# Next inputs by quarters, an ELU end and difference sums at later places, and later chunk loads in a fused retention and ELU kernel

## The chip, the cores and the metric

The kernel runs on one core of one Trainium2 chip. The metric is device time in microseconds for one launch; lower is better. Every run of a kernel gives one time, and a kernel is told by the median of its runs. One further execution is recorded by the hardware profiler, and the profile and the trace come from it.

The engines are named as the profile names them: PE is TensorE (matmuls; PEld are its weight loads), DVE is VectorE, ACT is ScalarE, POOL is GpSimd, and SP is SyncE, whose queue issues the DMAs here. "L921" is line 921 of the kernel before.

## What is computed

The reference, cut to what matters:

```python
def _attn_ref(q, k, v):                      # each (4, 8, 768, 64)
    gamma = 1.0 - 2.0 ** (-5.0 - np.arange(H))
    scale = 1.0 / np.sqrt(D)
    for t in range(S):
        state = gamma * state + einsum('bhd,bhe->bhde', k[:, :, t], v[:, :, t])
        y[:, :, t] = scale * einsum('bhd,bhde->bhe', q[:, :, t], state)

def _moe_ref(x, w_in, w_out):                # (3072, 512), (512, 2048), (2048, 512)
    h = x @ w_in
    g = np.where(h > 0.0, h, np.exp(np.minimum(h, 0.0)) - 1.0)
    return g @ w_out
```

A retention (linear attention with decay, 4 batches, 8 heads, 768 steps, head size 64) gives 3072 tokens of 512 numbers; a layer to 2048, an ELU and a layer back to 512 follow. All of it is float32.

## The kernel before

**Tiling.** The 3072 tokens are worked on in six blocks of 512 (`tb` 0 to 5), each made of four chunks of 128 tokens. A chunk's q, k and v are one load of 1 MB (`load`, L113) into one of four buffers, and its v is scaled on GpSimd soon after the load (`scale_v`, L289). Retention is done chunk by chunk with 64x64 matmuls: scores (L315), masked by VectorE (L326), states (L355, summed by L367), and outputs (L411 and L426, with a small read `seen`, L395, between their two halves, and L401 that writes the result into the input `x` of the first layer).

**Strassen.** The two layers use Strassen's scheme in Winograd's form: seven products of half-sized blocks instead of eight, with sums and differences before and after. Written with a first operand in quarters a11, a12, a21, a22 and a second in b11, b12, b21, b22, product 1 reads b11, 2 reads b21, 3 reads b22, and 4, 5, 6 and 7 read four differences. They are always done in the order 1, 2, 6, 7, 5, 3, 4. Products that share a sum accumulate in the same bank of PSUM: `pa` takes 1, 6, 5 and 3, `pb` takes 2, `pd` takes 7 and 4. Between two products of one bank the partial result must be read out: by a copy on ScalarE from `pa`, by an add on VectorE from `pb` and `pd`. `pa` has two buffers, `pb` and `pd` one each. So a product into `pd` waits until VectorE has read what stood there.

**Two levels.** Blocks 1 to 5 use the scheme twice. The outer level has products `j` in the order 1, 2, 6, 7, 5, 3, 4 (`ORDER2`), and each of them is again seven inner products `k`. The input of an outer product is one of the five arrays `C11`, `C12`, `C21`, `C22` and `T3` (`INPUT2`; `T1` lies in the place of `C12`). Outer product 1 reads C11. Then C11 is overwritten in place: by T3 + C11 for outer product 6, and later by C21 - C11 for outer product 4. That is `next_input` (L790) for block 1, and `next_big_input` (L1202) for the large groups. Within an outer product, inner products 1, 2 and 3 read quarters of the array itself (b11, b21, b22; quarter b12 is read by VectorE alone), and four differences of its quarters are made on VectorE (L879) for inner products 4 to 7.

**Stages in order of time.** Block 0 runs to 130 us or so. Block 1 goes through the first layer in four parts `first(n)` (to 182 us) and through the second in `second_twice` (182 to 243 us, products on L909, sums on L921). Blocks 2 and 3 form the first large group (`nb` = 0), blocks 4 and 5 the second (`nb` = 1). Each large group goes through `big_twice` (products on L1122, sums on L1137), `big_rest` (L1170, sums on L1183) and `second_big` (products on L1222, sums on L1234; 350 to 454 us and 544 to 632 us). While one block is in its layers, the retention of the next ones is slipped in between (`retention_step`), except in the second large group, behind which nothing follows.

**What sets the order.** The program writes its instructions out by hand, with Python generators: an engine executes its own instructions in the order in which the generators emit them, and semaphores order them across engines. `inner(j)` emits products 1 and 2; then 6 and 7; then 5; then 3; then 4, and stops after each of these. The loop of `second_twice` and `second_big` takes outer product `j` through its first steps, then lets the outer product before finish its inner products 3 and 4 (`before`), then yields "first", and so on; "middle" comes between inner products 7 and 5 of `j`, and `j` itself after 5. The main program reacts to these yields with retention steps (`VISITS`) and chunk loads (`LOADS`), both keyed by (step, place), where a step is one outer product. The four chunks of block 3 are loaded during `second_twice`.

**The ELU.** `elu` (L489) emits two instructions on ScalarE, which make exp(min(h, 0)), and puts the third, on VectorE (L498), on a list `later`, so that VectorE needn't wait for ScalarE. `depth` says how many entries the list may hold before its oldest are emitted; `flush` emits all.

**Weights of the second layer.** They lie in DRAM, already combined, and come through a ring of eleven slots of 256 KB (`wq`; eight of them remain for the large groups). An inner product's `done` gives its slot back and `fetch` issues the next load (L821) at once on SyncE's queue. That queue is in order: a DMA that waits for its buffer holds up all DMAs that stand behind it. Chunk loads (L113) and stores of results (L950, L1297) go through the same queue.

**Differences of the first layer's inputs.** For a large group, `big_x` and `big_layer_x` make the differences of inputs (L879 and L1092). They are parts of one generator `xparts`, of which the main loop takes some at a time. `big_end` for C11 (L1183) adds the bank `qa` to it.

Of the kernel before, what the change touches and what calls it, by code (L numbers as in the profile page):

```python
# [19 lines left out]
def kernel(  # L20
# [728 lines left out]
    def first(n):  # L749
# [17 lines left out]

        def use(name, h):
            flat = lambda x: x.rearrange("p a b -> p (a b)")
            elu(flat(mine(name)), flat(h))  # L770
            if name == "C12":

                sub = lambda o, x, y: nc.vector.tensor_tensor(out=o, in0=x, in1=y, op=ALU.subtract)
                later.append(lambda: sub(mine("T3"), mine("C22"), mine("C12")))
                later.append(lambda: sub(mine("T1"), mine("C12"), mine("C11")))
# [9 lines left out]
    def next_input(j):  # L785

        x, op = {2: ("T3", ALU.add), 6: ("C21", ALU.subtract)}[j]
        for n in range(NQ):
            q = slice(2 * n, 2 * n + 2)
            nc.vector.tensor_tensor(out=gq["C11"][:, q], in0=gq[x][:, q], in1=gq["C11"][:, q], op=op)  # L790

# [94 lines left out]
    def second_twice(tb, behind_last):  # L888
# [88 lines left out]
        for at, j in enumerate(ORDER2):  # L977
            cur = inner(j)
            next(cur)
            if j == 1:  # L980
                yield "tail"
            for _ in before:
                pass
            if at:
                yield "first"
            if j == 2:
                flush()
                next_input(2)
            if j == 5:
                next_input(6)  # L990
            if j == 1:

                next(cur)
                yield "elu"
                next(cur)
            parts = input_parts(ORDER2[at + 1]) if at + 1 < 7 else iter(())
            if j in (2, 5):

                next(parts)
            else:  # L1000
                for _ in parts:
                    pass
            if at == 6:
                behind_last()
            if j != 1:
                next(cur)
                yield "middle"
                next(cur)
            for _ in parts:
                pass  # L1010
            before = cur
            yield j
        for _ in before:
# [183 lines left out]
    def next_big_input(j):  # L1197

        x, op = {2: ("T3", ALU.add), 6: ("C21", ALU.subtract)}[j]
        for r in range(2):  # L1200
            for q in (slice(0, 2), slice(2, 4)):
                nc.vector.tensor_tensor(out=G["C11"][r][:, q], in0=G[x][r][:, q], in1=G["C11"][r][:, q], op=op)  # L1202

    def second_big(nb, behind_last):
        quarter = lambda x, r, t: G[x][r][:, :, TH * t : TH * t + TH]
# [118 lines left out]
        for at, j in enumerate(ORDER2):  # L1324
# [6 lines left out]
            if at:  # L1331
                yield "first"
            if j == 2:
                flush()
                next_big_input(2)
            if j == 5:
                next_big_input(6)
            if j == 1:

                next(cur)  # L1340
# [14 lines left out]
                next(cur)  # L1355
            for _ in parts:
                pass
            before = cur
            yield j
        for _ in before:  # L1360
# [242 lines left out]
    flush()  # L1603
    retention_step(2, 2)
    step, VISITS = 0, {(0, "end"): 3, (1, "first"): 4}
    LOADS = {(0, "end"): 0, (1, "middle"): 1, (2, "end"): 2, (4, "middle"): 3}
    for s in sec:
        if s == "first":
            step += 1
# [16 lines left out]
    for nb in range(NB):  # L1626
# [23 lines left out]
        for at, (j, sub) in enumerate(ORDER1):  # L1650
# [4 lines left out]
            if at:  # L1655
                next(tail, None)
            else:
                run(tail)
            next(cur)
            run(tail)  # L1660
            if at == 1 and nb == 0:
# [12 lines left out]
                    retention_step(3, 4)  # L1674
                some(xparts, 4)
            elif at == 2:
                some(xparts, 2)
                if more:
                    bring(groups[0], 0)
            elif at == 3:  # L1680
                run(xparts)
                if more:
                    bring(groups[0], 1)
            if nb == 0:
                stores[at]()
                send_small()
            if at == 2:
                first_c11 = big_end(0, "C11", qa[0])
        next(tail)
        first_c11()  # L1690

        sec = second_big(nb, (lambda: run(big_x(2))) if more else lambda: None)
# [117 lines left out]
```

## Time and profile before

| what | value |
|---|---|
| median of 3 runs | 637.15 us (636.79 to 638.11) |
| the profiled execution's own time | 635.8 us |
| its span, first to last instruction | 634.0 us |
| granted clock of TensorE | 1.00 of full speed, throughout |
| instructions | 13048 |
| read from and written to HBM | 90.96 MB and 28.05 MB |
| weight fetches (L821) | 183 of 256 KB, 3.1 us from issue to landing (median) |
| chunk loads (L113) | 22 of 1 MB, 7.3 us (median) |
| L921, L790 and L1202 on VectorE | 0.28, some 0.62 and some 1.13 us each |

A busy time in the profile is the time in which an engine had an instruction under way. Matmuls are pipelined and their ends are modelled, so a matmul looks busy a little longer than it keeps the next one from starting; the pace from start to start is the better measure. "Idle before" is the time for which an engine did nothing before an instruction, and what stands behind an arrow is what ended that time. A wait for several semaphores is put down to the one that came last. In the timeline, equal instructions that follow each other are put together as "x8"; a float32 matmul counts twice there.

### The profile page before, as it was taken

What the parts mean: (1) busy time and instruction counts of PE and PEld (TensorE: products, weight loads), DVE (VectorE), ACT (ScalarE), POOL (GpSimd) and SP (SyncE); (2) the same over time, 40 slices, a digit from 0 to 9 for tenths busy, and PEclk for the clock granted to TensorE, in tenths of its full rate; (3) what the DMA queues carried; (4) which work ended last, traced back from release to release, by engine and by line L of the source; (5) the groups of instructions that cost most, each with busy time, mean ns of one, the idle gap of its engine ahead of it and who ended that gap; (6) DMA issues with size and microseconds to landing.
All of it is one profiled execution on the core that took longest, in us unless ns stands there. A gap on an engine that the chain in (4) does not pass through costs nothing.

```text
span 634.0 us, 13048 instructions
## 1 busy us (share of the span) xinstructions
PE 619.3 (98%) x5350; PEld 464.5 (73%) x5350; DVE 469.5 (74%) x730; ACT 246.0 (39%) x420; POOL 25.2 (4%) x30
## 2 busy tenths in 40 slices
PE   8999999999999989999999999999999999999997
PEld 5864578888888988764454788888875444688886
DVE  5679789989886785656787986776455777895683
ACT  6798646025541112147657301010236666511110
POOL 1012000000000110010100003000000000000000
PEclk9999999999999999999999999999999999999999
DMA  8698669689464996499000249454643222456552
GB/s 324 253 411 295 182 204 269 196 266 303 152 207 128 385 389 214 141 304 304 34 4 0 84 154 353 169 154 138 201 132 100 67 84 76 135 154 184 152 178 84
DMA packets 73578, 119.85 MB, mean 189 GB/s; under 512 B 5552, under 2 KB 42672, under 8 KB 68784
## 3 DMA queue, kind: packets, MB, share of 16 engines
q1 hardware_dynamic: 73520, 119.04, 57.0%
q8 instruction: 42, 0.69, 0.4%
q14 instruction: 16, 0.13, 0.1%
HBM read 90.96 MB, written 28.05 MB: 188 GB/s over the span
## 4 chain that ended last, share of the span: by engine, by line
PE 90%; DMA 4%; DVE 4%; issue 1%; ACT 0%; SPq 0%; DVEq 0%
PE pa L1222 15%; PE pa L1170 11%; PE pd L1222 7%; PE pb L1170 4%; PE pa L761 4%; PE pb L1222 4%; PE pa L1122 4%; DMA wq<-scratch_dram 3%; PE pa L538 3%; PE x L628 3%; PE pd L1170 3%; PE pa L628 2%; PE pd L1122 2%; PE y L411 2%; PE sc L315 2%; PE pd L761 2%
## 5 line engine op out<-in xcount | busy, mean ns | idle before, releaser
L495 ACT ACTIVATE r<-r 128x512 f32<-128x512 f32 x96 | 60.5, 630 | 3.1
L1230 ACT COPY ms<-pa 128x256 f32<-128x256 f32 x41 | 15.3, 372 | 116.3 <-PE pa L1222 116.3
L1222 PE MATMUL pa<-gC,wq 128*128 128x256 f32 x160 | 38.5, 384 | 0.0
L1234 DVE TENSOR_TENSOR res<-pd,ms 128x256 f32<-128x256 f32 x26 | 11.0, 421 | 35.7 <-PE pd L1222 32.5
L289 POOL TENSOR_TENSOR chunk<-chunk,vf 128x512 f32<-128x512 f32 x16 | 22.3, 1393 | 359.5 <-DMA chunk<-in_qkv_dram 342.1
L1222 PEld LDWEIGHTS pa<-gC,wq 128*128 128x128 f32 x160 | 29.8, 190 | 5.1 <-issue 1.0
L1222 PE MATMUL pa<-ts,wq 128*128 128x256 f32 x112 | 26.5, 379 | 0.0
L1222 PE MATMUL pd<-ts,wq 128*128 128x256 f32 x112 | 26.5, 379 | 0.0
L1170 PE MATMUL pa<-ts,wq 128*128 128x512 f32 x56 | 26.3, 592 | 0.0
L707 ACT COPY m<-pa 128x512 f32<-128x512 f32 x26 | 15.1, 580 | 27.7 <-PE pa L1170 9.6
L1222 PEld LDWEIGHTS pa<-ts,wq 128*128 128x128 f32 x112 | 21.3, 190 | 3.3 <-issue 0.5
L1222 PEld LDWEIGHTS pd<-ts,wq 128*128 128x128 f32 x112 | 21.3, 190 | 2.9
L1222 PE MATMUL pa<-w_s,wq 128*128 128x256 f32 x96 | 22.5, 379 | 0.0
L1133 ACT COPY m<-pa 128x512 f32<-128x512 f32 x16 | 9.4, 585 | 31.2 <-PE pa L1122 31.2
L494 ACT ACTIVATE r<-gC 128x512 f32<-128x512 f32 x24 | 14.9, 621 | 15.2 <-DVE gC L1183 15.2
L1170 PEld LDWEIGHTS pa<-ts,wq 128*128 128x128 f32 x56 | 10.6, 190 | 13.4 <-issue 13.4
L1222 PEld LDWEIGHTS pa<-w_s,wq 128*128 128x128 f32 x96 | 18.2, 190 | 2.9 <-issue 0.5
L1256 ACT COPY res<-pa 128x256 f32<-128x256 f32 x13 | 4.8, 372 | 38.1 <-PE pa L1222 38.1
L917 ACT COPY ms<-pa 128x128 f32<-128x128 f32 x21 | 5.6, 265 | 35.2 <-PE pa L909 34.6
L1183 DVE TENSOR_TENSOR gC<-pa,gC 128x512 f32<-128x512 f32 x20 | 13.8, 689 | 5.8 <-PE pa L1170 5.5
L909 PE MATMUL pd<-ts,wq 128*128 128x128 f32 x112 | 15.2, 278 | 2.8 <-DVE res L921 1.5
L498 DVE SCALAR_TENSOR_TENSOR gC<-r,gC 128x512 f32<-128x512 f32 x24 | 17.5, 729 | 0.3 <-ACT r L495 0.3
(375 smaller groups left out, 1496.9 us busy)
## 6 DMA issues: line engine op xcount, KB each, us to landing
wq<-scratch_dram SPq DMA_DIRECT2D x183, 256.0 KB, 3.1
chunk<-in_qkv_dram SPq DMA_DIRECT2D x22, 1024.0 KB, 7.3
wraw<-in_w_dram SPq DMA_DIRECT2D x15, 1024.0 KB, 6.1
scratch_dram<-gT SPq DMA_DIRECT2D x12, 256.0 KB, 4.3
out_dram<-res SPq DMA_DIRECT2D x5, 512.0 KB, 3.1
scratch_dram<-m SPq DMA_DIRECT2D x12, 192.0 KB, 6.0
scratch_dram<-so SPq DMA_DIRECT2D x4, 512.0 KB, 4.7
scratch_dram<-wi SPq DMA_DIRECT2D x8, 256.0 KB, 6.6
```

The source lines that it names most:

```text
L289: eng.tensor_tensor(out=v, in0=v, in1=vf[:, i].unsqueeze(2).to_broadcast([C, H, D]), op=ALU.mult)
L495: nc.scalar.activation(e, e, AF.Exp, scale=-1.0)
L498: nc.vector.scalar_tensor_tensor(g, e, -1.0, h, ALU.add, ALU.max)
L538: nc.tensor.matmul(hp, lhsT=w[n][:, fi, j // 2, j % 2, :], rhs=xb[:, j, :], start=(j == 0), stop=(j == 3))
L628: nc.tensor.matmul(X[j][:, d, :], lhsT=w[j][:, d * P : d * P + P], rhs=x[j], start=(n == 0 and d == 0), stop=at_end, skip_group_check=True,)
L707: nc.scalar.copy(m, ps)
L761: nc.tensor.matmul(ps[:, fi, :], lhsT=w[:, fi, j2, :], rhs=x[:, j2, :], start=(begin and fi == 0 and j2 == 0), stop=(j2 == 1), skip_group_ ...
L909: nc.tensor.matmul(ps, lhsT=w[:, f, :], rhs=ts[j][k][:, f, :], start=(begin and f == 0), stop=(f == 3), skip_group_check=True,)
L1122: nc.tensor.matmul(ps[:, f, :], lhsT=w[:, f, :], rhs=big_xs[j][k], start=(begin and f == 0), stop=True, skip_group_check=True,)
L1170: nc.tensor.matmul(ps, lhsT=w[:, k, :], rhs=layer_x[j][:, 2 * k : 2 * k + 2, :], start=(j in (1, 7) and k == 0), stop=(k == 1), skip_group ...
L1222: nc.tensor.matmul(ps, lhsT=w[:, f, :], rhs=ts[j][k][:, f, :], start=(begin and f == 0), stop=(f == 3), skip_group_check=True,)
L1230: nc.scalar.copy(m, ps)
```

## The change

Five things are moved. No arithmetic is added or left out; the in-place sums are cut in another way.

1. `first` calls `elu` with a depth of 2 instead of 1 for its last part (`n` = 3), so that its ELU ends stay on the list for one call longer.
2. `next_input` and `next_big_input` become generators. They work on C11 quarter by quarter, in the order b11, b12, b21, b22, and not on four runs of whole rows. For outer product 6, three quarters (all but b22, which inner product 3 of outer product 1 still reads) are emitted at the end of step `j` = 1, and the last at the old place in step `j` = 2. For outer product 4, two quarters are emitted at the end of step 7 and two at the end of step 5; before, all four stood in step 5.
3. `flush` moves along, from step 2 to the end of step 1.
4. The loads of block 3's four chunks go to later places of `second_twice`.
5. In a large group, two of the four differences of `big_layer_x` and the `big_end` of C11 move from the end of round `at` = 2 to round `at` = 3, behind the sum that the round before still had to make from its `pd`; the last difference moves to behind the loop.

On the engines, only the order on VectorE and on SyncE's queue changes, and with it some semaphore waits. TensorE, ScalarE and GpSimd execute the same instructions in the same order.

```diff
@@ -767,7 +767,7 @@

         def use(name, h):
             flat = lambda x: x.rearrange("p a b -> p (a b)")
-            elu(flat(mine(name)), flat(h))
+            elu(flat(mine(name)), flat(h), 2 if n == NQ - 1 else 1)
             if name == "C12":

                 sub = lambda o, x, y: nc.vector.tensor_tensor(out=o, in0=x, in1=y, op=ALU.subtract)
@@ -785,9 +785,11 @@
     def next_input(j):

         x, op = {2: ("T3", ALU.add), 6: ("C21", ALU.subtract)}[j]
-        for n in range(NQ):
-            q = slice(2 * n, 2 * n + 2)
-            nc.vector.tensor_tensor(out=gq["C11"][:, q], in0=gq[x][:, q], in1=gq["C11"][:, q], op=op)
+        for r in range(2):
+            for t in range(2):
+                mine = lambda x: gq[x][:, 4 * r : 4 * r + 4, P * t : P * t + P]
+                nc.vector.tensor_tensor(out=mine("C11"), in0=mine(x), in1=mine("C11"), op=op)
+                yield

@@ -984,10 +986,9 @@
             if at:
                 yield "first"
             if j == 2:
-                flush()
-                next_input(2)
-            if j == 5:
-                next_input(6)
+                run(changes)
+            if j == 7:
+                changes = next_input(6)
             if j == 1:

                 next(cur)
@@ -1008,6 +1009,12 @@
                 next(cur)
             for _ in parts:
                 pass
+            if j == 1:
+                flush()
+                changes = next_input(2)
+                some(changes, 3)
+            elif j in (7, 5):
+                some(changes, 2)
             before = cur
             yield j
         for _ in before:
@@ -1198,8 +1205,10 @@

         x, op = {2: ("T3", ALU.add), 6: ("C21", ALU.subtract)}[j]
         for r in range(2):
-            for q in (slice(0, 2), slice(2, 4)):
-                nc.vector.tensor_tensor(out=G["C11"][r][:, q], in0=G[x][r][:, q], in1=G["C11"][r][:, q], op=op)
+            for t in range(2):
+                mine = lambda x: G[x][r][:, :, TH * t : TH * t + TH]
+                nc.vector.tensor_tensor(out=mine("C11"), in0=mine(x), in1=mine("C11"), op=op)
+                yield

     def second_big(nb, behind_last):
         quarter = lambda x, r, t: G[x][r][:, :, TH * t : TH * t + TH]
@@ -1331,10 +1340,9 @@
             if at:
                 yield "first"
             if j == 2:
-                flush()
-                next_big_input(2)
-            if j == 5:
-                next_big_input(6)
+                run(changes)
+            if j == 7:
+                changes = next_big_input(6)
             if j == 1:

                 next(cur)
@@ -1355,6 +1363,12 @@
                 next(cur)
             for _ in parts:
                 pass
+            if j == 1:
+                flush()
+                changes = next_big_input(2)
+                some(changes, 3)
+            elif j in (7, 5):
+                some(changes, 2)
             before = cur
             yield j
         for _ in before:
@@ -1603,7 +1617,7 @@
     flush()
     retention_step(2, 2)
     step, VISITS = 0, {(0, "end"): 3, (1, "first"): 4}
-    LOADS = {(0, "end"): 0, (1, "middle"): 1, (2, "end"): 2, (4, "middle"): 3}
+    LOADS = {(1, "first"): 0, (2, "end"): 1, (4, "end"): 2, (5, "end"): 3}
     for s in sec:
         if s == "first":
             step += 1
@@ -1656,6 +1670,9 @@
                 next(tail, None)
             else:
                 run(tail)
+            if at == 3:
+                some(xparts, 2)
+                first_c11 = big_end(0, "C11", qa[0])
             next(cur)
             run(tail)
             if at == 1 and nb == 0:
@@ -1674,19 +1691,16 @@
                     retention_step(3, 4)
                 some(xparts, 4)
             elif at == 2:
-                some(xparts, 2)
                 if more:
                     bring(groups[0], 0)
             elif at == 3:
-                run(xparts)
                 if more:
                     bring(groups[0], 1)
             if nb == 0:
                 stores[at]()
                 send_small()
-            if at == 2:
-                first_c11 = big_end(0, "C11", qa[0])
         next(tail)
+        run(xparts)
         first_c11()

         sec = second_big(nb, (lambda: run(big_x(2))) if more else lambda: None)
```

## The prediction

> **What bounds the kernel now.** I read the page first: how busy TensorE is, and whose work the chain that ended last is.
>
> ```profile
> PE 619.3 (98%) x5350; PEld 464.5 (73%) x5350; DVE 469.5 (74%) x730; ACT 246.0 (39%) x420; POOL 25.2 (4%) x30
> ...
> PE 90%; DMA 4%; DVE 4%; issue 1%; ACT 0%; SPq 0%; DVEq 0%
> ```
>
> TensorE is busy 98% of 634.0 us and 90% of the chain. The change leaves its instructions and their order alone, so it can only give back TensorE's waits, or add some. The waits, by line and releaser:
>
> ```profile
> PE pd L1122 <- DVE gT L1137: 1.7, 2, 0.9
> PE pd L909 <- DVE res L921: 1.5, 2, 0.9
> ...
> PE pa L909 <- DMA wq<-scratch_dram: 1.1, 1, 1.1
> PE y L426 <- issue: 1.0, 1, 1.0
> PE pd L909 <- DVE h L712: 0.8, 1, 0.8
> ...
> PE pd L909 <- DMA wq<-scratch_dram: 0.5, 1, 0.5
> ```
>
> These are measured from the modelled end of the matmul before. Measured from start to start they are some 0.17 larger: a product of line 909 normally takes 0.89 us and one of L1122 0.86. By the timeline, the product begun at 189.83 is 0.98 late, the one at 208.19 0.81, 215.24 0.70, 223.71 1.26, 236.42 1.03, 275.87 1.03 and 474.07 0.95. All but the last two lie in the stage of 182 to 243 us (`second_twice`). After each wait for VectorE the next matmul comes another 0.10 late.
>
> One such wait in the timeline (start, duration, engine):
>
> ```profile
> 203.40 2.49 DVE L790 TENSOR_TENSOR gC<-gT,gC 128x512 f32<-128x512 f32 x4
> ...
> 205.86 1.53 POOL L289 TENSOR_TENSOR chunk<-chunk,vf 128x512 f32<-128x512 f32 x1 [153.92 <-DMA chunk<-in_qkv_dram]
> ...
> 206.52 1.42 DVE L879 TENSOR_TENSOR ts<-gC,ts 128x512 f32<-128x512 f32 x1
> ...
> 207.86 0.28 DVE L921 TENSOR_TENSOR res<-pd,ms 128x128 f32<-128x128 f32 x1
> ...
> 208.19 1.16 PE L909 MATMUL pd<-ts,wq 128*128 128x128 f32 x8 [0.65 <-DVE res L921]
> ```
>
> L921 empties the bank `pd`; it stands in VectorE's queue behind the next inputs (L790), and behind an L879 that GpSimd's L289 stretched from 0.69 to 1.42. The DMA waits have their origin in SyncE's own waits:
>
> ```profile
> SPq L821 <- DMA wq<-scratch_dram: 8.1, 22, 1.4
> SPq L113 <- PE y L426: 7.1, 1, 7.1
> ```
>
> A chunk load stood for 7.1 us at the head of the queue, until 200.99, while four weight slots came free behind it. Two stretches show it (length, then busy time and count of PE, PEld, DVE, ACT and POOL, clock, share of the DMAs in use, GB/s):
>
> ```profile
> 196.40:201.00 4.60, 4.60 (x85) 4.42 (x87) 1.13 (x6) 0.53 (x2) 0.00 (x0) 1.00 0.02 4
> 201.00:235.00 34.00, 31.74 (x297) 30.86 (x290) 27.36 (x49) 5.04 (x19) 4.38 (x4) 1.00 0.98 365
> ```
>
> The DMAs stand still at 0.02, then run full at 0.98. Weights land 6 to 9 us after issue (2.6 before), until two products wait for theirs.
>
> **The change, place by place** (times of the profile of before).
>
> *The ELU end* (L498, one every 0.60). One moves from before the seven L367 to behind the L921 of the first product, another from there to behind the L712 that empties `pd`. The L712 that starts at 189.09 then starts at 188.49; its bank is complete at 188.13, so nothing else is late. Gain 0.60 of the 0.98. The rest stays, for one L498 still stands ahead. The first L498, moved behind four L326 and an L289, has no reader before 176.
>
> *Inputs by quarters, `second_twice`, j = 2.* Four L790 take 2.49. Three go to 196.7, ahead of two L395, and end some 1.87 later, at 198.6. There VectorE idles 1.68 before the L921 of 198.62 and 1.43 before that of 200.34, so this is hidden; without that idle time it would cost up to 1.87. One stays: L879 then starts 1.87 earlier, at 203.9, and the L921 of 207.86 at about 205.3, before TensorE wants `pd` (207.38): gain 0.81 + 0.10. The two products begun at 204.13 and 205.34, which followed L790 step by step (1.21 and 1.15 instead of 0.89), give 0.32 + 0.26 = 0.58.
>
> *j = 6.* Two quarters go to 220.2 (idle 0.7 and 1.4 there), two to 228.4. The L921 sums of 222.66 and 230.24, which wait for TensorE themselves, aren't moved. Cost 0.
>
> *Chunk loads.* On SyncE the first goes behind four weight fetches, the second behind eight more and a store, the third behind fourteen, the fourth behind eight and a store. The four fetches are released by products that end from 197.6 to 200.3, and run while the DMAs idle. From there a fetch takes 0.67 of the full DMAs by the pace at which they land (0.72 by 262 KB at 365 GB/s), a product 0.89, a chunk load, four times as large, some 2.6. After the first load nine products follow until the second, fourteen until the third, seven until the fourth; each wins back 0.22, and the two stores cost 0.67 each. The backlog runs 2.6, 1.3, 3.9, 0.8, 3.4, 2.5, 5.1, while the full ring leads by ten products, 8.9, less 2.6 to land: 6.3. So the weights are on time: gain 0.70 + 1.26. At 0.72 the last figure would be 7.8, a wait of 1.5; the lower bound is a gain of 0.46.
>
> *The scaling on GpSimd* (L289, same order) follows its chunk. The third load now goes out behind the fetch released at the end of the product begun at 225.57, near 226.6, where the fourth was. With the 4.7 that the chunk of 200.99 took, L289 starts near 231.3. VectorE works without a pause from 230.24 to 236.3 (three adds of L921, four L879, the L921 that empties `pd`). The product of 236.42 was late because L289 lay there too: the last L879 took 1.54 instead of 0.69. So I leave this wait in place, at 0.85 + 0.1, and count a gain of 0.1; bounds 0 and 1.03 (L289 beside the chain).
>
> Rows of before: VectorE lost 0.73, 0.84 and 0.85 to an L289. The Trainium skill (SBUF — State Buffer, "Who interferes with whom") says that a VectorE instruction with two SBUF inputs and a GpSimd one that reads SBUF exclude each other for the whole instruction. By that the loss could be all of an undisturbed L289, 1.04, and the sum 0.2 worse; I take the rows.
>
> *L1137 ahead of two L1092 and an L1183:*
>
> ```profile
> 272.27 1.22 DVE L1092 TENSOR_TENSOR gC<-xb,gC 128x1024 f32<-128x1024 f32 x1
> ...
> 275.14 0.68 DVE L1137 TENSOR_TENSOR gT<-pd,m 128x512 f32<-128x512 f32 x1
> ...
> 275.87 1.13 PE L1122 MATMUL pd<-ts,wq 128*128 128x256 f32 x4 [0.87 <-DVE gT L1137]
> ```
>
> `pd` is complete at 273.3, so L1137 ends by 274.1, ahead of the 274.84 at which TensorE wants the bank. What is late next: both L1092 by some 1.65 (the later ends at 276.2, wanted near 281), L1183 (276.9, wanted at 278.4) and the L1137 of `pb` (277.5, wanted at 281). Gain 1.03 + 0.10, and in the second group 0.95 + 0.10: 2.18.
>
> *Inputs by quarters, `second_big`.* Four L1202 take 4.62, so 1.13 from one to the next. Three now stand ahead of the L1234 that empty `pb` and `pd`. First group: L879 ends at 365.96; three quarters 3.40, two L395 0.15, an L1234 0.33, the L1234 of `pd` 0.42: 370.26. TensorE wants `pd` at 370.74: no wait, 0.48 to spare. The L395 of 376.49 comes earlier, and a 0.25 hitch of L426 at 376.77 goes. The second group has no retention work on TensorE in between:
>
> ```profile
> 558.55 1.22 DVE L879 TENSOR_TENSOR w_s<-w_a,ts 128x1024 f32<-128x1024 f32 x1
> 559.68 0.42 DVE L1234 TENSOR_TENSOR res<-pb,ms 128x256 f32<-128x256 f32 x1
> ...
> 561.18 0.42 DVE L1234 TENSOR_TENSOR res<-pd,ms 128x256 f32<-128x256 f32 x1 [1.08 <-PE pd L1222]
> ...
> 562.71 1.89 PE L1222 MATMUL pd<-w_s,wq 128*128 128x256 f32 x8
> ```
>
> 559.68 + 3.40 + 0.33 + 0.42 = 563.83, and the product of 562.71 starts at about 563.87: **a new wait** of 1.16 + 0.10. Behind this L1234 stand only the fourth quarter and L879 for a product 3.4 us off. The other quarters lie in idle time (592.1 to 594.0 and 605.6 to 607.6).
>
> A quarter in place, 128x4x256, has no row. Below: 1.13 (L1202, same elements, and L1092 into 4x256 slots of `w_s`); above: 2.06, the longest 128x1024 of VectorE (an L879 beside L289). I take 1.13, the row without GpSimd, which is idle there.
>
> **Sum.** 0.60 + 0.91 + 0.58 + 1.96 + 0.1 + 2.18 + 0.25 = 6.6 gained, 1.26 lost: 5.3. Span 634.0 becomes 628.7; that execution's own 635.8 becomes 630.5. The median shown is 637.15, 1.35 above it, so 631.8.
>
> **Rivals.**
> - *The new wait does not come, or the third L289 misses the chain.* For: the first group shows that a half us decides. Against: VectorE is gapless from 555.0 on. 1.26 and 0.9 better: 629.8 to 630.6.
> - *Weights stay late; the loads merely move the crowd.* For: the same bytes run through 182 to 243. Against: the DMAs idled before 201. It keeps 1.5 to 1.96, perhaps a wait more in front of L1122: 633.3 to 635.
> - *The change doesn't do what it says: waits return one for one* behind the moved work: 636 to 638.4. Against: idle time stands at each new place but one.
> - *Slower: quarters in place are dear.* They stand ahead of the emptying sums in both groups. At x us each the second group waits 1.16 + 3(x - 1.13), the first 3(x - 1.13) - 0.48; that eats all 6.6 from about x = 2.1. At 2.5: 5.27 + 3.63 + 0.2 = 9.1, so 639.7. For: no row of this form. Against: L1092 into 4x256 slots at 1.22.
>
> **How the numbers follow.** Forecast 0.52 (its own range 630.7 to 633.3); better 0.15; late weights 0.19; one for one 0.04; slower 0.10. About 0.2%, 1.3 us, can't be told from no change. Faster 0.86, same 0.04, slower 0.10. Range 629.8 to 634.9: it leaves out the last two and a little at either end.
>
> **What would show it.** The wait of `pd` for L1137 gone twice; both waits of L909 for `wq` gone and fetches landing in 2.6 to 5; one wait of L909 for L921 left, beside an L289; a new wait of L1222 for L1234 near 557. Wrong, if waits for `wq` remain, if the wait near 557 is missing, or if a quarter takes clearly over 1.2.

## The result, and the profile after

The changed kernel takes 631.23 us, the median of 4 runs (630.98 to 631.34); before, run beside it, took 636.97 (635.13 to 638.11). The ratio is 0.9912, with a 95% interval of 0.9888 to 0.9936. The profiled execution took 631.13 us, with a span of 629.4, against 635.8 and 634.0.

The page of the kernel after (busy time of each engine, and the shares of the chain that ended last):

```profile
PE 617.8 (98%) x5350; PEld 463.7 (74%) x5350; DVE 468.9 (75%) x730; ACT 246.0 (39%) x420; POOL 23.1 (4%) x30
...
PE 90%; DMA 4%; DVE 3%; issue 1%; ACT 0%; SPq 0%; DVEq 0%
```

The engines do the same work as before. What changed is in TensorE's waits (line, releaser: total, times, longest):

```profile
...
PE pd L1231 <- DVE res L1243: 1.0, 1, 1.0
PE y L411 <- issue: 0.9, 1, 0.9
PE y L426 <- issue: 0.8, 1, 0.8
...
PE pd L911 <- DMA wq<-scratch_dram: 0.3, 1, 0.3
...
PE pd L911 <- DVE h L712: 0.2, 1, 0.2
PE pa L911 <- DMA wq<-scratch_dram: 0.2, 1, 0.2
```

(Lines have moved: L909 is now L911, L921 L923, L790 L791, L879 L881, L821 L823, L1122 L1129, L1137 L1144, L1170 L1177, L1183 L1190, L1202 L1210, L1222 L1231 and L1234 L1243.) The waits for L1137 and L921 have left the list, and those for weights fell from 1.6 to 0.5. New are the wait for L1243 that the prediction announced, and a longer stall of L411 at "issue".

TensorE executes the same 5350 matmuls in the same order, so each one's start can be held against its own start in before. Wherever the difference steps, time was won or lost. Places with steps of 0.1 us or more, their steps summed up ("start" sums several, of -0.5 to +0.8, ahead of 29 us):

```
place (before)  step      what it is                              predicted
start           -0.2
189.83          -0.62     ELU end (L712)                          -0.60
196.21          -0.21     a stall at issue is shorter
204.1 to 206.2  -0.60     products in step with L790              -0.58
208.19          -0.91     wait for L921 gone                      -0.91
215.24, 223.71  -1.21     weights: -0.76, -0.94, then +0.49       -1.96
236.42          -0.86     last L879 beside L289                   -0.1
258 to 262      +0.55     stall at issue: -0.55, then +1.10
275.87, 474.07  -2.23     waits for L1137 gone                    -2.18
295.7, 297.5    +0.69     new waits of L1177
376.77          -0.26     hitch of L426                           -0.25
562.71          +1.28     new wait for L1243                      +1.26
sum             -4.6                                              -5.3
```

The timeline of the kernel after shows the place of the first fence of the prediction again (start, duration, engine):

```profile
202.34 0.68 DVE L791 TENSOR_TENSOR gC<-gT,gC 128x512 f32<-128x512 f32 x1
...
204.27 0.28 DVE L923 TENSOR_TENSOR res<-pd,ms 128x128 f32<-128x128 f32 x1
204.47 0.68 DVE L881 TENSOR_TENSOR ts<-gC 128x512 f32<-128x512 f32 x1
...
205.73 0.72 PE L911 MATMUL pd<-ts,wq 128*128 128x128 f32 x5
```

One quarter stands where four instructions stood. The L923 that empties `pd` starts at 204.27 instead of 207.86, well ahead of the product at 205.73, which has no wait any more. The stretches of the DMAs, again for the kernel after (length; busy time and count of PE, PEld, DVE, ACT and POOL; clock, DMA share, GB/s):

```profile
195.40:199.90 4.50, 4.50 (x82) 4.37 (x84) 2.99 (x8) 0.53 (x2) 0.00 (x0) 1.00 0.43 115
199.90:235.00 35.10, 34.68 (x332) 34.10 (x323) 27.36 (x53) 5.61 (x21) 3.14 (x3) 1.00 0.98 353
```

Where the DMAs stood at 0.02 they now carry 0.43: the four weight fetches that were stuck behind the chunk load. Afterwards they are as full as before. In the DMA view from 199 to 240 us, the weight fetches need 6.5 us from issue to landing (median of 33):

```profile
wq<-scratch_dram SPq DMA_DIRECT2D x33, 256.0 KB, 6.5
```

The sums of the large groups, kernel after:

```profile
269.24 0.69 DVE L1144 TENSOR_TENSOR gT<-pd,m 128x512 f32<-128x512 f32 x1 [0.97 <-PE pd L1129]
...
269.85 1.22 DVE L1099 TENSOR_TENSOR gC<-xb,gC 128x1024 f32<-128x1024 f32 x1
...
270.77 1.03 PE L1129 MATMUL pd<-ts,wq 128*128 128x256 f32 x4
```

L1144 stands ahead of the difference, and `pd` is empty 0.84 before TensorE asks for it. And the new wait:

```profile
553.80 3.49 DVE L1210 TENSOR_TENSOR gC<-w_b,gC 128x1024 f32<-128x1024 f32 x3
...
557.21 0.42 DVE L1243 TENSOR_TENSOR res<-pb,ms 128x256 f32<-128x256 f32 x1
557.54 0.42 DVE L1243 TENSOR_TENSOR res<-pd,ms 128x256 f32<-128x256 f32 x1
...
558.01 1.99 PE L1231 MATMUL pd<-w_s,wq 128*128 128x256 f32 x8 [1.02 <-DVE res L1243]
```

Three quarters in 3.41 (553.80 to 557.21) are 1.14 each. They stand ahead of two sums, and TensorE waits 1.02 for the second.

### The profile page after: what moved, and what is told of

It reads as the page before. It is cut to its first block, busy times and chain, and to the rows that moved or that the text cites. A ratio compares the mean times of both kernels' runs of the same rounds, so it can differ in the third digit from the quotient of the medians.

```text
span 629.4 us, 13050 instructions
## 1 busy us (share of the span) xinstructions
PE 617.8 (98%) x5350; PEld 463.7 (74%) x5350; DVE 468.9 (75%) x730; ACT 246.0 (39%) x420; POOL 23.1 (4%) x30
## 4 chain that ended last, share of the span: by engine, by line
PE 90%; DMA 4%; DVE 3%; issue 1%; ACT 0%; SPq 0%; DVEq 0%
PE pa L1231 14%; PE pa L1177 10%; PE pd L1231 7%; PE pa L1129 5%; PE pa L761 4%; PE pb L1177 4%; PE pb L1231 4%; PE pa L538 3%; PE x L628 3%; PE pa L911 3%; PE pd L1177 3%; PE pd L1129 2%; PE pa L628 2%; PE y L411 2%; PE pd L761 2%; PE sc L315 2%
## 5 line engine op out<-in xcount | busy, mean ns | idle before, releaser
L1243 DVE TENSOR_TENSOR res<-pd,ms 128x256 f32<-128x256 f32 x26 | 11.0, 422 | 39.0 <-PE pd L1231 27.4
L1231 PE MATMUL pa<-gC,wq 128*128 128x256 f32 x160 | 38.5, 384 | 0.0
L1231 PEld LDWEIGHTS pa<-gC,wq 128*128 128x128 f32 x160 | 29.8, 190 | 5.1 <-issue 1.0
L289 POOL TENSOR_TENSOR chunk<-chunk,vf 128x512 f32<-128x512 f32 x16 | 20.1, 1258 | 357.1 <-DMA wq<-scratch_dram 177.6
L1231 PE MATMUL pd<-ts,wq 128*128 128x256 f32 x112 | 26.5, 379 | 0.0
L1231 PE MATMUL pa<-ts,wq 128*128 128x256 f32 x112 | 26.5, 379 | 0.0
L1177 PE MATMUL pa<-ts,wq 128*128 128x512 f32 x56 | 26.3, 592 | 0.0
L707 ACT COPY m<-pa 128x512 f32<-128x512 f32 x26 | 15.1, 581 | 28.0 <-PE pa L761 15.7
L1231 PEld LDWEIGHTS pa<-ts,wq 128*128 128x128 f32 x112 | 21.3, 190 | 3.3 <-issue 0.5
L1231 PEld LDWEIGHTS pd<-ts,wq 128*128 128x128 f32 x112 | 21.3, 190 | 2.9
L1231 PE MATMUL pa<-w_s,wq 128*128 128x256 f32 x96 | 22.5, 379 | 0.0
L1177 PEld LDWEIGHTS pa<-ts,wq 128*128 128x128 f32 x56 | 10.6, 190 | 13.4 <-issue 13.4
L1231 PEld LDWEIGHTS pa<-w_s,wq 128*128 128x128 f32 x96 | 18.2, 190 | 2.9 <-issue 0.5
L1190 DVE TENSOR_TENSOR gC<-pa,gC 128x512 f32<-128x512 f32 x20 | 13.8, 689 | 5.9 <-PE pa L1177 5.6
L498 DVE SCALAR_TENSOR_TENSOR w_a<-r,w_a 128x512 f32<-128x512 f32 x16 | 11.9, 742 | 7.5 <-ACT r L495 7.5
L498 DVE SCALAR_TENSOR_TENSOR gC<-r,gC 128x512 f32<-128x512 f32 x24 | 17.3, 720 | 0.1
```

The source lines that it names most:

```text
L289: eng.tensor_tensor(out=v, in0=v, in1=vf[:, i].unsqueeze(2).to_broadcast([C, H, D]), op=ALU.mult)
L498: nc.vector.scalar_tensor_tensor(g, e, -1.0, h, ALU.add, ALU.max)
L707: nc.scalar.copy(m, ps)
L1177: nc.tensor.matmul(ps, lhsT=w[:, k, :], rhs=layer_x[j][:, 2 * k : 2 * k + 2, :], start=(j in (1, 7) and k == 0), stop=(k == 1), skip_group ...
L1231: nc.tensor.matmul(ps, lhsT=w[:, f, :], rhs=ts[j][k][:, f, :], start=(begin and f == 0), stop=(f == 3), skip_group_check=True,)
```

## Experiments

Twelve kernels, each run beside before on the same chip (medians of before: 636.8 to 637.2). The kernel after was run apart from them, so what is said against its 631.23 compares medians of different groups:

| kernel | is | median us (runs) | ratio to before, 95% interval |
|---|---|---|---|
| `loads_only` | before + loads | 634.77 (9) | 0.9955 (0.9937 to 0.9973) |
| `all_but_loads` | after - loads | 635.67 (11) | 0.9981 (0.9970 to 0.9993) |
| `twice_quarters_only` | before + quarters of `second_twice` | 636.32 (10) | 0.9987 (0.9973 to 1.0001) |
| `elu_only` | before + ELU end | 635.83 (12) | 0.9987 (0.9971 to 1.0002) |
| `sums_only` | before + sums | 634.89 (10) | 0.9971 (0.9954 to 0.9988) |
| `big_quarters_only` | before + quarters of `second_big` | 638.16 (10) | 1.0022 (1.0006 to 1.0038) |
| `one_quarter_first` | after, two quarters later | 630.22 (5) | 0.9897 (0.9881 to 0.9914) |
| `stores_first` | after, stores ahead of a load | 631.07 (5) | 0.9918 (0.9898 to 0.9939) |
| `best` | both of these | 629.90 (6) | 0.9904 (0.9872 to 0.9936) |
| `more_blanks` | after, 33 blank products | 635.13 (11) | 0.9971 (0.9954 to 0.9989) |
| `best_fewer` | `best`, 17 blank products | 633.42 (6) | 0.9948 (0.9928 to 0.9967) |
| `split_scale` | before, one L289 in two | 636.80 (12) | 0.9991 (0.9976 to 1.0007) |

### The loads, alone and left out

```diff
-    LOADS = {(0, "end"): 0, (1, "middle"): 1, (2, "end"): 2, (4, "middle"): 3}
+    LOADS = {(1, "first"): 0, (2, "end"): 1, (4, "end"): 2, (5, "end"): 3}
```

`loads_only` makes this edit in before:

> The kernel before with the four later chunk loads alone. Theory (the loads work by themselves, through the DMAs and through the place of GpSimd's L289): both waits of L909 for wq shrink from 0.70 and 1.26 us to at most 0.75 together, the wait of the product that comes fourth in outer product 2 (0.81) loses the 0.7 that L289 adds to the L879 before it, and the wait of 1.03 at the end of the stage goes, since the third L289 falls behind VectorE's chain; 2.5 to 3 us faster, 634.2. Rival (the loads only move the crowd, and gain with the quarters alone): the waits for wq return at other products with 1.5 us or more, at most 0.7 us faster, 636.3 or more.

`all_but_loads` takes it back in after:

> The kernel after, with the chunk loads of the second large group at the places that they had before. Theory: the weights' waits come back whole: about 0.9 + 1.0 + 0.7 us and more at the places of 205.7 to 220.8, since the gains ahead of them (0.6 + 0.6 + 0.9 at the ELU and the quarters) only make TensorE arrive earlier at transfers that land when they did: 2 to 3.5 us slower than the kernel after, 633.2 to 634.7. Rival: the places of the loads matter little and the quarters brought the gain of this stage: less than 1 us slower.

Alone the loads gain 2.06 us (634.77 against 636.83), a little less than was expected, with steps of -0.72 at 208.19, -1.66 at the weights and -0.85 at 236.42: both parts of the theory are there, and the rival's 0.7 is passed. (In the profile, longer stalls at issue take 2.3 of this back, at 24.93 and 261.74.) Left out, they cost 4.4 (635.67 against 631.23), more than was expected. The waits of TensorE in `all_but_loads`:

```profile
PE pa L911 <- DMA wq<-scratch_dram: 1.6, 2, 1.4
...
PE pd L911 <- DMA wq<-scratch_dram: 1.4, 1, 1.4
```

Weights cost 3.0 here, 0.5 in the kernel after and 1.6 in before. So the ELU and the quarters, which bring TensorE forward by 2.1 us ahead of this place, only make it arrive earlier at weights that land when they did. In sum the shifts of this stage hold 3.5 of the 4.4; a wait of L1177 for L707 near 295 holds 0.48.

### What lies ahead of the weights, alone

`twice_quarters_only` (changes 2 and 3 in `second_twice`):

```diff
             if j == 2:
-                flush()
-                next_input(2)
+                run(changes)
...
+            if j == 1:
+                flush()
+                changes = next_input(2)
+                some(changes, 3)
```

> The kernel before with the quarters and the earlier flush of the second layer of block 1 alone (next_input). Theory (VectorE's queue): the two products that read the new C11 run at 0.89 us again (0.58 gained), the wait of 0.81 + 0.10 for L921 goes, the waits for wq stay at 1.9 to 2.2 us, for TensorE now asks for the weights earlier and they land as before, so that up to all of the 1.5 us gained ahead of them is given back: 0 to 0.8 us faster, 636.4 to 637.1. Rival (weights are paced by TensorE, so what is gained ahead of them stays): 1.4 to 1.5 us faster, 635.6.

```diff
-            elu(flat(mine(name)), flat(h))
+            elu(flat(mine(name)), flat(h), 2 if n == NQ - 1 else 1)
```

> The kernel before with the ELU's last part alone cut in two, as in the kernel after. Theory: TensorE's wait for L712 at 189.83 shrinks by 0.60 us, and the 0.6 us is given back to the waits for wq between 215 and 224, which end when transfers land: time 0 to 0.3 us faster than before, 636.5 to 636.8. Rival: what is gained there stays to the end: 0.6 us faster, 636.2.

Both show their own steps (-0.59 and -0.91; -0.60) and both give them back between 211 and 226 us: `twice_quarters_only` with +0.83 and +0.89, `elu_only` until its shift against before is -0.01 at 225.68. Neither interval excludes 1. The theory held in the profiles. (Both also have a shorter wait at 236.42, by 0.86 and 0.59, which neither edit was made for; see the section on the lock.) `elu_only`'s profiled execution spans 634.1, as before's 634.0; that its median is 1 us lower, more than expected, isn't explained by a step of the trace.

### The sums, and the two waits that nobody ordered

```diff
+            if at == 3:
+                some(xparts, 2)
+                first_c11 = big_end(0, "C11", qa[0])
...
             elif at == 2:
-                some(xparts, 2)
...
-                run(xparts)
...
-            if at == 2:
-                first_c11 = big_end(0, "C11", qa[0])
         next(tail)
+        run(xparts)
```

> The kernel before with the moved differences and C11 sum of the first layer alone (L1137 ahead of L1092 and L1183). Theory: both waits of L1122 for L1137 go, 1.03 and 0.95 us with 0.10 of slow restart each, but in the first large group some 0.6 to 0.7 us come back near 291 us as two waits of L1170 (for L707 and for L1183), since the store of w_a that L1183 waits for is paced by DMAs and not by TensorE: 2.1 less 0.65, 1.4 to 1.5 us faster, 635.5. Rival (the wait near 291 us comes from the chunk loads or the quarters of the stage before): no wait at L1170, 2.1 to 2.2 us faster.

Steps of -1.13 and -1.09, as expected; 634.89 against 636.83. Of the +0.69 that after shows at 295.7 and 297.5, only +0.12 came. The theory had 0.6 to 0.7 of it coming back here; that was wrong, so it isn't the sums' own price. The chain, in the timeline of the kernel after:

```profile
287.65 0.69 DVE L1190 TENSOR_TENSOR w_a<-pb,m 128x512 f32<-128x512 f32 x1 [4.80 <-DMA scratch_dram<-w_a]
...
288.97 0.63 ACT L494 ACTIVATE r<-w_a 128x512 f32<-128x512 f32 x1 [2.80 <-DVE gC L498]
...
290.17 0.57 ACT L707 COPY m<-pd 128x512 f32<-128x512 f32 x1
...
290.79 0.30 PEld L1177 LDWEIGHTS pd<-ts,w_b 128*128 128x128 f32 x2 [0.92 <-ACT m L707]
```

L1190 may not overwrite `w_a` before its store has landed; behind it wait L498, the ELU on ScalarE, the copy L707 in ScalarE's queue, and TensorE. In before the wait for the store was 3.7. `stores_first` sends the stores ahead of the chunk load that stood before them:

```diff
-            elif at == 3:
-                if more:
-                    bring(groups[0], 1)
             if nb == 0:
                 stores[at]()
                 send_small()
+            if at == 3 and more:
+                bring(groups[0], 1)
```

> The kernel after, with the stores of w_a and w_s issued ahead of the second chunk load of the next large group. Theory: the two waits of L1177 at 290.8 and 292.8 (0.26 and 0.23 us, and 0.10 behind each) come from L1190, which waited 4.80 us for a store of w_a to land, because a chunk load stood ahead of the store in the queue. With the store ahead of it L1190 waits less than 3.7 us and both waits go: 0.7 us faster than the kernel after, about 630.5. Rival: the store is late because all DMA engines are full, whatever stands ahead: the two waits stay, and the time is within 0.3 us of the kernel after.

L1190 now waits 2.1, and both waits of TensorE are gone (-0.26, -0.23, and -0.10 behind each). But the time is that of the kernel after: 631.07. Other steps came: +0.32 at 302 and some +0.8 between 393 and 402. Ahead of 302 an L289 that now starts at 294.41 stretched an L498 from 0.68 to 0.97; in `best_fewer`, where L289 misses that L498, the step is gone. Of the +0.8, the first +0.30 is a product (at 393.39, here at 395.28) that starts 0.13 behind the landing of a weight fetch, which took 10.2 us behind two chunk loads. The other +0.47 stand behind an L881 that a later L289 stretched. Timeline of `stores_first`, GpSimd and then VectorE:

```profile
394.36 1.76 POOL L289 TENSOR_TENSOR chunk<-chunk,vf 128x512 f32<-128x512 f32 x1 [1.54 <-DMA chunk<-in_qkv_dram]
```

```profile
395.13 2.07 DVE L881 TENSOR_TENSOR w_s<-gC 128x1024 f32<-128x1024 f32 x1
397.23 1.22 DVE L881 TENSOR_TENSOR w_s<-gT,w_s 128x1024 f32<-128x1024 f32 x1
```

The first L881 takes 2.07 instead of 1.22. In the kernel after, L289 is through by 391.98 and L881 starts at 393.53, undisturbed. (The profiled execution of `stores_first`, 633.56, is the longest of its five: 1.7 us of the difference were lost ahead of 30 us, 0.5 in the stall at 257.67.)

### The new wait in the second large group

`big_quarters_only` makes changes 2 and 3 in `second_big` alone, in before.

> The kernel before with the quarters of the second layer of the large groups alone (next_big_input). Theory (three quarters ahead of the sums that empty pb and pd): a wait of 1.16 us with 0.10 of slow restart in the second large group near 562.7 us, the hitch of 0.25 at 376.77 gone, nothing else: 1.0 us slower, 638.0. Rival (the quarters gain in the large groups too, and the new wait is caused by something else in the whole change): no wait of L1222 for L1234, 0 to 0.3 us faster.

The step of +1.18 and +0.10 at 562.71 came, and -0.23 at 376.77. At 404 there was another +0.79 that wasn't expected: an L879 took 2.07 beside an L289. The kernel is slower than before by 1.3 us (638.16 against 636.83). `one_quarter_first` leaves one quarter ahead of the sums and puts two behind:

```diff
             if j == 1:
...
-                some(changes, 3)
+                some(changes, 1 if ends else 3)
```

> The kernel after, with one of the three quarters of the first 128 rows' change ahead of the sums that empty a bank, and the other two behind them. Theory: the wait for L1243 that stands at 558.01 (1.18 us and 0.10 of a restart behind it) is VectorE's work ahead of those sums: three quarters of 0.42 to 0.48 us each and one more ahead of them. With two of them gone (0.8 to 0.9 us) the sums end before TensorE asks for the bank or up to 0.4 us behind: the wait falls to 0 to 0.4, and the time by 0.8 to 1.28, to about 630.2. Rival: the quarters that now stand behind the sums come late for the transposes that read them, and a wait of about as much shows there: time within 0.3 us of the kernel after.

VectorE in `one_quarter_first`:

```profile
554.54 1.22 DVE L1210 TENSOR_TENSOR gC<-w_b,gC 128x1024 f32<-128x1024 f32 x1
555.67 0.42 DVE L1243 TENSOR_TENSOR res<-pb,ms 128x256 f32<-128x256 f32 x1
556.04 0.42 DVE L1243 TENSOR_TENSOR res<-pd,ms 128x256 f32<-128x256 f32 x1
```

The sum that empties `pd` ends at 556.46, and TensorE starts the product at 557.57 without a wait: step -1.19 and -0.10 against the kernel after, and nothing is late behind it. The quarters were sized wrongly in the expectation (0.42 to 0.48 are the sums; a quarter is 1.14), which made it too small at its lower end. The median fell by 1.0, but the intervals of the two ratios overlap, so the trace shows the gain and the medians alone don't prove it.

### Stalls at issue

Most profiles have stalls at "issue" in the dense 64x64 matmuls near 25, 195 and 258 us, 0.3 to 1.6 long from start to start. In the fourteen profiles all of them but one end 2.2 to 2.6 us after a 16 KB packet of the instruction queue starts (for example 193.77 and 196.21 in before; 192.86 and 195.16, 255.33 and 257.67 in after); the other, the short one of before at 258.33, ends 2.75 after. `more_blanks` shifts TensorE's instruction stream by eight matmuls that work on nothing:

```diff
-    for n in range(25):
+    for n in range(33):
```

> The kernel after, with eight more of the blank products that warm TensorE up ahead of the first loads, so that all later TensorE instructions stand eight places further on in its instruction stream. Theory: the stalls that the profile puts down to issue (1.29 us near 195 and 1.1 us near 257.7 in the kernel after) lie where a fetch of instructions comes too late, and so move or change by more than 0.3 us each when the stream is shifted, with no change of the same size in any wait for data. Rival: they belong to the work at these places (a crowd on the DMA engines), and stay at the same lines with the same length within 0.3 us. The time: within 1 us of the kernel after by either.

Waits of TensorE in `more_blanks`:

```profile
PE kv L355 <- issue: 1.4, 1, 1.4
...
PE pa L514 <- issue: 0.9, 1, 0.9
PE y L426 <- issue: 0.7, 1, 0.7
```

The stall of L411 at 258 shrank by 0.8 (1.10 to 0.32 from start to start), and two new ones came at 12.85 and 25.25, in lines that had none. `best_fewer` goes the other way, `range(17)`, in the kernel `best`:

> The kernel best with eight blank products fewer, so that later TensorE instructions stand eight places earlier in the stream. In more_blanks the stall of 1.1 us near 258 fell to 0.3 and two new ones of 1.1 and 1.6 us came at 12.9 and 25.3. If stalls at issue go by the place in the stream, they move again here: at least one of the two in best (near 195 and 258) changes by over 0.3 us, or a new one of over 0.5 us comes. Rival: the stalls stay as in best within 0.3 us, and more_blanks's were chance. The time by either within 2 us of best, with no sign foretold.

There one stall of 2.2 from start to start stands at 28.7, and the one at 196 is gone.

The lengths don't decide between theory and rival: in kernels whose TensorE stream isn't shifted at all, the stall near 258 is 0.4 (before) to 1.65 long (`stores_first`), and the one near 25 is missing (after) or up to 1.41 long (`loads_only`). The places do. Counted in TensorE's matmul records from 0, the stalls of the twelve unshifted kernels stand ahead of records 475, 2132 and 3006 or 3007 (in before 2879). The eight blank products are sixteen records, so in the shifted kernels the same numbers belong to other matmuls; yet the stalls stand ahead of 222, 475 and 2132 in `more_blanks` and ahead of 475 in `best_fewer`. Record 475 is in L411 in the kernel after and in L355 in `more_blanks`. So the stalls go with the place in the instruction stream, not with the work; which of the places stalls, and for how long, changes from execution to execution. That the times would be within 1 and 2 us was wrong: 3.9 above the kernel after and 3.5 above `best`. The profiled execution of `more_blanks` is only 1.75 longer (632.88); what its other runs, up to 638.29, lost was not seen. Eight of its eleven runs have a mean granted clock of 0.995 to 0.997, one of four of the kernel after. A stretch of 3.4 us at half the clock, as seen below in `best`, takes 0.003 from the mean by estimate, so some of the loss may be such stretches.

### The lock between VectorE and GpSimd

In several profiles the wait at 236.42 was gone though nothing near it was edited. Starts and durations of the L289 there and of the last L879 of four, from the traces (us):

```
kernel                L289 starts  L879 starts  L289 took  L879 took
before                     234.57       234.62       1.04       1.54
sums_only                  235.11       235.40       1.27       1.53
best                       235.36       235.57       1.20       1.53
split_scale                235.73       235.69       1.55       0.68
big_quarters_only          235.21       235.11       1.49       0.69
twice_quarters_only        236.19       235.96       1.35       0.68
all_but_loads              234.89       234.61       1.31       0.68
after                      231.38       230.86       1.06       0.69
```

Whoever asks first runs, and the other waits: an L879 takes up to 0.86 us longer, an L289 up to 0.51. (In `sums_only` and `best`, L289 came while the third L879 still ran, and so waited a little itself.) In before 0.05 us decided it against VectorE, in `split_scale` 0.03 us for it. `split_scale` was meant to test the lock itself:

```diff
+        for lo, hi in ((0, 1), (1, H)) if m == 3 * CPB + 2 else ((0, H),):
+            eng.tensor_tensor(
+                out=v[:, lo:hi], in0=v[:, lo:hi],
+                in1=vf[:, i, lo:hi].unsqueeze(2).to_broadcast([C, hi - lo, D]), op=ALU.mult,
+            )
```

> The kernel before, with the third L289 of the second large group made in two instructions, one head (64 columns) first and the other seven behind. In before this L289 (1.04 us) started 0.05 us ahead of the fourth L879, which then took 1.54 us in place of 0.69. Theory: the two engines exclude each other, the lock goes to whoever asked first and is given up after every instruction: wherever L289 starts, no L879 there takes over 0.95 us, and TensorE's wait at 236.42 falls by 0.6 to 0.86 us; the time by as much, to about 636.1. Rival: the lock stays with GpSimd while it has work, and L879 takes 1.5 us again if the first piece starts ahead of it: wait and time as before.

I split the wrong one: the L289 of 234.57 belongs to the fourth chunk, the third's is at 223. So TensorE's wait was not tested; it vanished by the order of the starts alone. At 223 the trace still answers the question of the lock (VectorE's L792 is the old L790, GpSimd's L290 the old L289):

```
DVE  L792 222.996 took 0.679     POOL L290,  64 columns 223.126 took 0.698
DVE  L792 223.595 took 0.779
DVE  L792 224.298 took 1.418     POOL L290, 448 columns 223.789 took 1.378
```

The first piece waits for the first L792, the second L792 loses 0.10 to it, the second piece waits for the second L792, and the third L792 loses 0.74. The lock changes hands after every instruction, in the order of asking. VectorE lost 0.84 in all, as in before, so splitting gained nothing, and "no add over 0.95 us" was wrong. The time is that of before.

### Both improvements together

> The kernel after with both edits that one_quarter_first and stores_first tried alone. Theory: they act at different places (558 and 290 to 293), so their steps at TensorE add: -1.28 and -0.69 us, 1.97 in all, about 629.3 us; the profile shows neither L1231 waiting for L1243 nor L1177 waiting for L707 or L1190. Rival: what one frees the other takes back, or the late chunk loads of stores_first cost again what they did there (0.3 to 0.5 us at 301.9 and near 400): 630.0 to 630.6.

The median of `best` is 629.90, with runs from 628.17 to 631.9 and one of 635.37, which is the one with the profile. Its steps against the kernel after at 558 (-1.28) and at 290.8 and 292.8 (-0.69) are there, as are the costs of `stores_first` at 302 and near 400 (+0.31 and +0.65). In this execution a product waited 2.16 us for weights at 223.04, the matmuls behind it ran slowly for another 1.6 (see the last section), and an L881 beside an L289 at 235.57 cost 0.84; no edit was made near these places. So the weights of this stage still come late by different amounts: in `best_fewer` TensorE doesn't wait for them at all. By the median it is the rival's case, 630.0 or a little less, and no more can be claimed: the intervals of `best`, `one_quarter_first` and the kernel after overlap.

## Why the prediction was right

- **Bound.** TensorE's waits were all there was to win, and the sum was one of waits. Its six large terms came within 0.05 us: the ELU end, the quarters' rate and the wait for L921 in `second_twice`, the waits for L1137, the hitch at 376.77, and the loss at 562.71. The slower rival fell with the quarters at 1.14 instead of 2.1 us.
- **Weights, mis-sized.** "So the weights are on time: gain 0.70 + 1.26" gave 1.21. The pace of 0.67 held: from 208.7 to 235.8 us in the kernel after, fetches that follow each other land 0.62 to 0.69 apart, but for three. What failed is the backlog ("The backlog runs 2.6, 1.3, 3.9"), from its first term on. The four early fetches landed up to 1.94 apart, the first chunk load landed 4.16 behind the last of them and not 2.6, and the first fetch behind it took 7.26 from issue: 4.7 above the 2.6 of a free queue. Some 2 us of this stayed: the longest fetch behind the second chunk load took 8.61, a backlog of 6.0 in place of 3.9. Two fetches there landed 1.10 and 1.39 behind the transfer before them, at 219.31 and 220.70, and the products that start 0.14 behind these landings are the two that are late, by 0.32 and 0.42. Why these landings lie further apart isn't shown. What the loads save is also more than the sum's term: with everything else changed and the loads left in place, 3.0 us of weight waits are there. The term for the weights can't be added to those for the ELU and the quarters: without it these gain nothing clear of the noise.
- **L289, mis-sized.** "I leave this wait in place ... and count a gain of 0.1": the gain was 0.86. The chunk was issued at 224.02, and by "the 4.7 that the chunk of 200.99 took" L289 would have started near 228.9, among the four L881 of 228.93 to 231.54. It took 7.1 to land, for the same full DMAs, and L289 came at 231.38, half a us behind the start of the last one. The bound of 1.03 held. The rival that named this case had it at 0.9.
- **Not foreseen.** The two waits of L1177 (+0.69) through a store that landed late, and the stalls at issue (+0.55 and -0.21).
- **Its own signs.** "Wrong, if waits for `wq` remain": two remain, short ones. Fetches don't land "in 2.6 to 5" but in 6.5, and the wait of L909 for L921 beside an L289, which was to be left, is gone. The signs at L1137, near 557 us and on the quarters came.
- **The base.** The sum made the span 628.7; it is 629.4. The median came out lower than the forecast because I added 1.35 for the distance of before's profiled execution to the median; after's is only 0.1 from its own.

The two errors of the sum, -0.75 and +0.76, cancel, and what was not foreseen is made up by the base. That the total is so close is partly luck.

## What to carry to other kernels

When several edits act ahead of one transfer-bound place, size them together: here two of them gained nothing clear of the noise until the loads moved, and the loads were worth twice as much with them. Ahead of a sum that empties a bank, count the instructions queued before it against the time at which TensorE wants the bank; that arithmetic held to 0.05 us, and it also tells how many may stay. A load moved in time moves whatever is done with its data: look up what that meets on the other engines, and take a place that a tenth of a us decides as a gamble in either direction.

## What the runs showed of the hardware

- **The lock goes by order of asking, for each instruction.** An add of two SBUF operands on VectorE lost up to 0.86 us to an L289 that asked before it. An L289 lost up to 0.5 to an add of 128x512, and 1.07 beside one of 128x1024 (397.13 in `big_quarters_only`, 2.11 in place of 1.04). The Trainium skill (SBUF — State Buffer, "Who interferes with whom") says that issue order decides who blocks, and that the loser waits for the whole instruction; the runs agree on the order, and the loss is somewhat less than the 1.04 that an undisturbed L289 takes.
- **TensorE's clock fell behind waits of 1.3 and 2.2 us, and not behind others as long.** In the profiled execution of `best`, a product waited 2.16 us for weights, and the next 3.4 us ran at half the clock, 0.21 us from matmul to matmul instead of 0.11. Stretches of `best` (columns as above):

```profile
220.60:223.00 2.40, 0.28 (x3) 0.08 (x1) 1.58 (x3) 0.00 (x0) 0.52 (x1) 1.00 1.01 385
223.00:226.50 3.50, 3.46 (x16) 3.50 (x17) 0.00 (x0) 0.27 (x1) 0.52 (x1) 0.51 0.82 282
```

  Sixteen matmuls cost some 1.6 us more, so the wait cost nearly double. The length of a wait alone doesn't decide. In the same execution a wait of 1.31 us, ended at 10.31, was followed by another stretch at half the clock, from 11.40 to 14.82; the waits of 1.4 us in `all_but_loads` and a stall of 1.97 at 28.73 in `best_fewer` were not. The Trainium skill (TensorE: Matmul & The Clock Gate, "What's actually happening") puts the fall after an idle window of some 3.4 us. Both stretches did last 3.41 us, but the 3.41 us ahead of them were not wholly idle: TensorE was busy for 1.26 us of those ahead of 223.03 and for 1.84 of those ahead of 11.40. What share of busy time decides isn't shown.
- **Eight empty matmuls at the start moved the time by 3.5 to 3.9 us**, up in both directions. Stalls at issue moved with them, of up to 2.2 us; they account for a part only, for the profiled execution of `more_blanks` is 1.75 longer, and where its other runs lost the rest isn't shown.
